# Linear attention with a gated layer behind it: the state's sum written in place in PSUM, the last three output steps in another order, and the last gate's product on VectorE

## The chip, the cores and the metric

The kernel runs on one core of a Trainium2 chip. The metric is the device time of one execution in microseconds, as the median of several. Five engines work beside each other, each with its own queue: TensorE (PE) multiplies matrices into PSUM, VectorE (DVE), ScalarE (ACT) and GpSimd (POOL) work element by element, and SyncE (SP) issues the DMAs. In this kernel GpSimd's operands all lie in SBUF; VectorE's and ScalarE's lie in SBUF or in PSUM.

## The reference, cut to what matters

B, H, S, D are 4, 8, 768, 48. The first part is a linear attention with a decaying state, the second a gated layer with a spatial mix over the sequence.

```python
state = zeros(B, H, D, D)
for t in range(S):
    cur = einsum('bhd,bhe->bhde', u[None] * kt, vt)
    y[:, :, t] = einsum('bhd,bhde->bhe', rt, state + cur)
    state = w[None, :, :, None] * state + einsum('bhd,bhe->bhde', kt, vt)
x = y.transpose(0, 2, 1, 3).reshape(B, S, H * D)          # 4 x 768 x 384

h = maximum(x @ w_in, 0.0)                                # 384 -> 1024
u, v = h[..., :512], h[..., 512:]
v_n = (v - mean(v)) / sqrt(var(v) + 1e-06)
v_s = einsum('ts,bsd->btd', w_spatial, v_n) + b_spatial[None, :, None]
out = (u * v_s) @ w_out                                   # 512 -> 384
```

## The kernel before, in words

**Attention.** Each of the 4 batches is cut into 6 chunks of 128 time steps, 24 chunks in all (`NM`), and each chunk into two halves of 64. Every chunk goes through these steps. `prep` (lines 237 to 275) scales r and k by powers of w: `scale` (L248 on GpSimd, L249 on VectorE; from chunk 8 on L251 on VectorE alone), `rku` and `ks` on GpSimd (L254, L255, L258), a sum over features `red` on VectorE (L261), and `dia` on GpSimd (L270). `g1` (L287, L296) makes on TensorE the products of k and r and of k and v into the PSUM tile `ps`, of which there is one buffer (two banks). `mid` (lines 306 to 327) takes the masked products out on VectorE (L310) and carries the state on: `ua` and `ub_` are the k-v products of the two halves, views of `ps`. L318 adds `ua` to the state `s` into `t1`, L325 adds `ub_`, and L326 multiplies by `w128`, which gives the state of the next chunk; the tile of each is 128 x 4 x 48 float32. ScalarE copies the state and `t1` into block form (L303, L304), which `g2` (L336) on TensorE uses to make the chunk's output. `fin` and `fin_low` (L366 on ScalarE, then either L376 on TensorE and L377 on ScalarE, or L368 on VectorE) split it into a high and a low part.

**The layer behind it.** Every product is made of three matmuls on high and low parts (`mm3`, L392 to L394): high by high, high by low, low by high. `moe_v` and `moe_u` make the two halves of the hidden layer, `moe_sp` mixes over the sequence and makes the gate, `moe_out` multiplies by w_out. In `moe_sp`, VectorE adds the bias (L479), GpSimd multiplies by u (L480), and then ScalarE and VectorE split the gate into a high and a low part (`split`, L172 and L173). In `moe_out`, 4 feature blocks of 3 matmuls each (12 in all) fill one PSUM tile `pm`, ScalarE copies it into the SBUF tile `ob` (L492), and SP stores it (L493). `pm` has four buffers, and `ob` has two.

**The order of the work.** Every engine runs its instructions in the order in which the program writes them out; no planner changes it. The loop at the end of `fused_kernel` (lines 542 to 587) writes, for each chunk, `g2`, `fin`, `g1` of the next chunk, `mid` of the next chunk, the loads of the chunk three further on, `prep` of the chunk two further on, and between these the steps of the layer from the list `steps` and pieces of the weights' preparation from the list `fill` (`pour`). In the first chunks (i < 6) the counts in `FIRST` and `POUR` say how many steps and pieces. The pieces (`from_f64`, lines 175 to 205) turn raw 64-bit weights into two float32 parts, mostly on VectorE (L183 to L203) with one copy on ScalarE (L200); `sp_pieces` does the same for the spatial weights. `later` and `tick` put a function behind so many steps; a gate's `split` follows its `moe_sp` at once. The last steps of the last batch (b = 3, t = 1) are the four `moe_sp` and then three `moe_out`, for 128 rows of the output each.

Of the kernel before, what the change touches and what calls it, by code (L numbers as in the profile page):

```python
# [7 lines left out]
F32 = mybir.dt.float32  # L8
# [3 lines left out]
ALU = mybir.AluOpType  # L12
AX = mybir.AxisListType

B, H, S, D = 4, 8, 768, 48
# [3 lines left out]
P = 128  # L19
# [4 lines left out]
NP = H // 2  # L24
NK = DM // P
NS = S // P
ND = DH // P
# [9 lines left out]
def fused_kernel(ctx, tc, rkT, rkvN, wT, uB, w_in, w_sp, b_sp, w_out, out):  # L37
    nc = tc.nc
# [16 lines left out]
    ps_m = ctx.enter_context(tc.tile_pool(name="ps_m", bufs=4, space=bass.MemoryType.PSUM))  # L55
# [15 lines left out]
    def raw_out(k):  # L71
        t = sm.tile([P, 2 * DM], U32, name="raw", tag="gt", bufs=5)
        raws["out", k] = t.rearrange("p (n k) -> p n k", k=2)
        src = w_out[k * P:(k + 1) * P, :]
        nc.sync.dma_start(out=raws["out", k], in_=src.bitcast(U32).rearrange("p (n k) -> p n k", k=2))

    def raw_sp(t, j):
        if t == 0:
            w = sm.tile([P, TH], F32, name="wst", tag="u", bufs=8)
        else:  # L80
            w = sm.tile([P, TH], F32, name="wst", tag="ob")
        raws["sp", t, j] = w
        nc.sync.dma_start(out=w, in_=w_sp[j * P:(j + 1) * P, t * TH:(t + 1) * TH])
# [40 lines left out]
    w128 = const.tile([P, NP], F32, name="w128")  # L124
# [27 lines left out]
    for n in range(2):  # L152
        t = const.tile([P, 2, NP, HC], F32, name=f"a{n}")
# [3 lines left out]
    for n in range(2):  # L157
        t = const.tile([P, NP, 2 * D], F32, name=f"sb{n}")
# [12 lines left out]
    def split(hi, lo, src, eng=None):  # L171
        nc.scalar.copy(hi, src)  # L172
        (eng or nc.vector).tensor_tensor(out=lo, in0=src, in1=hi.bitcast(F32), op=ALU.subtract)  # L173
# [128 lines left out]
    def block(dst, src):  # L302
        nc.scalar.copy(dst[0:64, :, 0:D], src[0:64])  # L303
        nc.scalar.copy(dst[64:P, :, D:2 * D], src[64:P])  # L304

    def mid(m):
        t, c = at[m], m % NC
        ps = t["ps"]
        ua, ub_ = (ps[:, i, 256:256 + NP * D].rearrange("p (n e) -> p n e", n=NP) for i in (1, 0))
        nc.vector.copy_predicated(out=t["a"], mask=mask_u.unsqueeze(1).unsqueeze(1).to_broadcast([P, 2, NP, HC]),  # L310
                                  data=ps[:, :, 0:256].rearrange("s j (p t) -> s j p t", p=NP))
        if c == 0:
            block(sblk[1], ua)
            t1 = ua
        else:
            block(sblk[0], st["s"])
            t1 = sm.tile([P, NP, D], F32, name="t1", bufs=1)
            nc.vector.tensor_tensor(out=t1, in0=st["s"], in1=ua, op=ALU.add)  # L318
            block(sblk[1], t1)
        if c < NC - 1:  # L320
            if c == 0:
                t1 = sm.tile([P, NP, D], F32, name="t1", bufs=1)
                nc.vector.tensor_copy(out=t1, in_=ua)
            s2 = sm.tile([P, NP, D], F32, name="s2")
            nc.vector.tensor_tensor(out=s2, in0=t1, in1=ub_, op=ALU.add)  # L325
            nc.vector.tensor_tensor(out=s2, in0=s2, in1=w128.unsqueeze(2).to_broadcast([P, NP, D]), op=ALU.mult)  # L326
            st["s"] = s2

    def g2(m):
        t, c = at[m], m % NC  # L330
        xp = ps_x.tile([P, 2, 512], F32, name="xp")
        t["xp"] = xp
        began = set()

        def mm(z, g, jt, lhsT, rhs):
            nc.tensor.matmul(xp[32 * g:32 * g + 32, z, jt * HC:(jt + 1) * HC], lhsT, rhs, start=(z, g) not in began,  # L336
                             stop=True, skip_group_check=True, tile_position=(ROWP[0], 32 * g))
            began.add((z, g))

        quads = [(jt, g, *((jt, g) if g < 3 else (3, jt))) for jt in range(NK) for g in range(4)]  # L340
        ROWP = [0]
        for z, s0, t0 in SUBS:
            if z == 0 and c == 0:
                continue
            for jt, g, p, k in quads:
                mm(z, g, jt, sblk[z][:, p, 32 * k:32 * k + 32], t["r"][:, p, t0:t0 + 64])
        parts = []
        for jt, g, p, k in quads:
            if k < 2:
                parts.append((jt, g, p, 0, 32 * k))  # L350
            if k > 0:
                parts.append((jt, g, p, 1, 32 * (k - 1)))
        for jt, g, p, j, e in parts:
            for z, s0, t0 in SUBS:
                ROWP[0] = s0
                mm(z, g, jt, t["v"][s0:s0 + 64, 2 * p + j, e:e + 32], t["a"][s0:s0 + 64, j, p, :])
# [25 lines left out]
    def later(n, f):  # L382
        due.setdefault(now[0] + n, []).append(f)

    def tick():
        now[0] += 1
        for f in due.pop(now[0], []):
            f()


    def mm3(o, lh, ll, rh, rl, first, last):
        nc.tensor.matmul(o, lh, rh, start=first, stop=False)  # L392
        nc.tensor.matmul(o, lh, rl, start=False, stop=False)  # L393
        nc.tensor.matmul(o, ll, rh, start=False, stop=last)  # L394
# [76 lines left out]
    def moe_sp(b, t, d):  # L471
        ds_ = slice(d * P, (d + 1) * P)
        ts_ = slice(t * TH, (t + 1) * TH)
        pm = ps_m.tile([P, 512], F32, name="pm")
        for s, vn in enumerate(vst[b]):
            mm3(pm[:, 0:TH], vn[:, 0, ds_], vn[:, 1, ds_], ws_h[:, s, ts_], ws_l[:, s, ts_], s == 0, s == NS - 1)
        u = us.pop((b, t, d))
        g = sm.tile([P, TH], F32, name="g", bufs=2)
        nc.vector.tensor_tensor(out=g, in0=pm[:, 0:TH], in1=bb[:, ts_], op=ALU.add)  # L479
        nc.gpsimd.tensor_tensor(out=g, in0=g, in1=u, op=ALU.mult)  # L480
        gt = sm.tile([P, 2, TH], F32R, name="gt", tag="gt", bufs=5)
        gs[b, t, d] = gt
        later(1, lambda: split(gt[:, 0], gt[:, 1], g))

    def moe_out(b, t, i):
        pm = ps_m.tile([P, 512], F32, name="pm")
        o = slice(i * P, (i + 1) * P)
        for d in range(ND):
            gt = gs[b, t, d]
            mm3(pm[:, 0:DM], gt[:, 0, o], gt[:, 1, o], wo_h[:, d, :], wo_l[:, d, :], d == 0, d == ND - 1)  # L490
        ob = sm.tile([P, DM], F32, name="ob", tag="ob")
        nc.scalar.copy(ob, pm[:, 0:DM])  # L492
        nc.sync.dma_start(out=out[b, t * TH + i * P:t * TH + (i + 1) * P, :], in_=ob)  # L493
# [3 lines left out]
    for b in range(B):  # L497
        v = [(moe_v, (b, c)) for c in range(NC)]
        u = [(moe_u, (b, t, d)) for t in range(2) for d in range(ND)]
# [30 lines left out]
    def pour(n):  # L530
        for _ in range(max(0, min(n, len(fill)))):
            fill.pop(0)()

    def sp_loads(t):
        for j in range(NS if t == 0 else 2):
            raw_sp(t, j)
        if t == 0:
            nc.sync.dma_start(out=bb, in_=b_sp)

    DMAS = {0: lambda: sp_loads(0), 2: lambda: [raw_out(k) for k in range(ND)], 3: lambda: sp_loads(1)}  # L540
    done = 0
    for i in range(-1, NM):
        if i < 0:
            parts = prep(0)
            for f in parts[0:2]:
                f()
            pour(4)
            for f in parts[2:]:
                f()
        else:  # L550
            g2(i)
            xs_all[divmod(i, NC)[0], i % NC // 3], *low = fin(i)
        if i < NM - 1:
            g1(i + 1)
        if i >= 0:
            fin_low(i, *low)
        if i < NM - 1:
            mid(i + 1)
        if i >= 0:
            load_chunk(i + 3)  # L560
        parts = prep(i + 2) if i < NM - 2 else []
        n = 0 if i < 0 else FIRST[i] if i < NC else len(steps) if i == NM - 1 else int(10 + (i - 5) * 28 / 6)
        p = POUR[i + 1] if i + 1 < len(POUR) else (0, len(fill))
        if i < NC:
            for _ in range(2):
                parts.pop(0)()
            pour(p[0])
            for f in parts:
                if f:
                    f()  # L570
            parts = []
        k = max(1, n - done)
        for j in range(k):
            pour(p[1] * (j + 1) // k - p[1] * j // k)
            if parts:
                parts.pop(0)()
            if done < n:
                f, args = steps[done]
                whole = {moe_v: 18, moe_u: 36, moe_sp: 42 if args[1] == 0 else 48, moe_out: 72}[f]
                pour(whole - 72 + len(fill))  # L580
                f(*args)
                done += 1
                tick()
        for f in parts:
            f()
        if i in DMAS:
            DMAS[i]()
    for _ in range(6):
        tick()

# [49 lines left out]
```

## Time and profile before

| | us |
|---|---|
| median of 3 runs (lowest, highest) | 379.31 (378.53, 379.43) |
| the profiled execution, its own time | 379.35 |
| its span, from the first to the last instruction | 377.5 |
| TensorE busy | 342.9 |
| VectorE busy | 215.9 |
| GpSimd busy | 152.5 |
| ScalarE busy | 145.3 |

The busy times are sums over the span; an engine that waits is not busy. A row of the time line gives an instruction's start and its duration, both in us, its engine, its line, what it writes and reads, and in brackets how long the engine had been idle and who ended that. A VectorE instruction's duration runs on while it is held up in the middle of its work, so two instructions of one shape and line can differ. Matmuls overlap: their starts, not their durations, say how fast they follow each other. "issue" is time for which the profile shows no other engine to wait for.

### The profile page before, as it was taken

The numbers are of one execution on the slowest core, as the hardware profiler recorded it, in microseconds if no ns is written. First come the engines' busy times: TensorE is split into PE (matmuls) and PEld (weight loads), VectorE is DVE, ScalarE is ACT, GpSimd is POOL, SyncE is SP. The second block draws the span as 40 slices with busy tenths as digits, with TensorE's granted clock in tenths as the row PEclk, the third lists the DMA queues.
The fourth block names the chain that finished last, engine by engine and source line by source line (L and its number), as shares of the span: only waits on it lengthen the run. The fifth ranks groups of instructions, "written<-read, shape, count | busy, mean of one in ns | idle before, by whom it ended". The sixth has DMA issues, their size and how long they took to land.

```text
span 377.5 us, 12269 instructions
## 1 busy us (share of the span) xinstructions
PE 342.9 (91%) x5459; PEld 314.1 (83%) x5459; DVE 215.9 (57%) x415; ACT 145.3 (38%) x320; POOL 152.5 (40%) x157
## 2 busy tenths in 40 slices
PE   2467669698999999999999999999999999999995
PEld 1456548597999998789899999889989998999994
DVE  6699975687855464577644445597444534443120
ACT  3033455756322333547313223647122335461212
POOL 5865745656265353421445273241563330003120
PEclk9996957989999999999999999999999999999999
DMA  7992933233303235303305314334031010000101
GB/s 260 417 387 92 322 144 130 82 129 129 129 2 129 73 129 180 120 20 133 115 2 180 110 71 152 128 104 150 5 127 65 4 44 25 0 0 2 42 21 64
DMA packets 14021, 41.69 MB, mean 110 GB/s; under 512 B 1680, under 2 KB 6416, under 8 KB 13968
## 3 DMA queue, kind: packets, MB, share of 16 engines
q1 hardware_dynamic: 13968, 40.90, 30.6%
q8 instruction: 43, 0.70, 0.8%
q14 instruction: 10, 0.08, 0.1%
HBM read 36.18 MB, written 4.72 MB: 108 GB/s over the span
## 4 chain that ended last, share of the span: by engine, by line
PE 81%; DVE 7%; DMA 3%; ACT 3%; issue 3%; POOL 2%; SPq 0%; POOLq 0%; DVEq 0%; ACTq 0%
PE pm L392 21%; PE pm L394 20%; PE pm L393 20%; PE xp L336 9%; PE ps L287 3%; PE ps L296 3%; DMA rkv<-rkvN 2%; DMA wst<-w_sp 2%; DVE rk L249 1%; PE pm L462 1%; PE pm L467 1%; PE pm L463 1%; DVE pm L199 1%; ACT vs L436 1%; DVE s L326 1%
## 5 line engine op out<-in xcount | busy, mean ns | idle before, releaser
L480 POOL TENSOR_TENSOR g<-g,u 128x384 f32<-128x384 f32 x32 | 32.5, 1016 | 118.0 <-DVE g L479 118.0
L392 PE MATMUL pm<-ws_h,vnorm 128*128 128x384 f32 x192 | 64.9, 338 | 0.0
L394 PE MATMUL pm<-ws_h,vnorm 128*128 128x384 f32 x192 | 64.2, 335 | 0.0
L393 PE MATMUL pm<-ws_l,vnorm 128*128 128x384 f32 x192 | 64.2, 334 | 0.0
L270 POOL TENSOR_TENSOR a<-diag,dg 128x512 f32<-128x512 f32 x24 | 25.4, 1059 | 86.0 <-DVE dg L261 56.1
L173 DVE TENSOR_TENSOR gt<-g,gt 128x384 fp32r<-128x384 f32 x32 | 21.0, 655 | 57.8 <-ACT gt L172 57.8
L172 ACT CAST gt<-g 128x384 fp32r<-128x384 f32 x32 | 16.4, 513 | 91.7 <-POOL g L480 91.7
L392 PEld LDWEIGHTS pm<-ws_h,vnorm 128*128 128x128 f32 x192 | 36.0, 188 | 0.3
L393 PEld LDWEIGHTS pm<-ws_l,vnorm 128*128 128x128 f32 x192 | 36.1, 188 | 0.0
L394 PEld LDWEIGHTS pm<-ws_h,vnorm 128*128 128x128 f32 x192 | 36.0, 188 | 0.0
L392 PE MATMUL pm<-wo_h,gt 128*128 128x384 f32 x96 | 33.0, 344 | 0.8 <-ACT gt L172 0.8
L394 PE MATMUL pm<-wo_h,gt 128*128 128x384 f32 x96 | 32.5, 338 | 0.4 <-issue 0.4
L393 PE MATMUL pm<-wo_l,gt 128*128 128x384 f32 x96 | 32.3, 336 | 0.0
L393 PE MATMUL pm<-wi_l,xh 128*128 128x512 f32 x72 | 29.6, 411 | 0.9 <-issue 0.9
L392 PE MATMUL pm<-wi_h,xh 128*128 128x512 f32 x72 | 30.2, 419 | 0.0
L394 PE MATMUL pm<-wi_h,xl 128*128 128x512 f32 x72 | 29.4, 408 | 0.0
L479 DVE TENSOR_TENSOR g<-pm,bb 128x384 f32<-128x384 f32 x32 | 17.7, 554 | 19.9 <-PE pm L394 19.8
L255 POOL TENSOR_TENSOR rkv<-rkv,ub 128x384 f32<-128x384 f32 x24 | 26.2, 1092 | 1.9
L336 PEld LDWEIGHTS xp<-rk,sb 128*32 128x32 f32 x1056 | 18.2, 118 | 9.8 <-issue 4.5
L413 DVE BATCH_NORM_STATS2 q<-vs 128x6 f32<-128x512 f32 x24 | 16.5, 687 | 16.6 <-ACT vs L406 16.6
L336 PE MATMUL xp<-a,rkv 64*32 64x64 f32 x1536 | 25.0, 234 | 0.0
L336 PE MATMUL xp<-rk,sb 128*32 128x64 f32 x1056 | 23.1, 234 | 2.1 <-ACT sb L303 2.1
(102 smaller groups left out, 733.7 us busy)
## 6 DMA issues: line engine op xcount, KB each, us to landing
rkv<-rkvN SPq DMA_DIRECT2D x24, 648.0 KB, 5.7
rk<-rkT SPq DMA_DIRECT2D x24, 512.0 KB, 4.1
out<-ob SPq DMA_DIRECT2D x24, 192.0 KB, 1.9
raw<-w_in SPq DMA_DIRECT2D x6, 512.0 KB, 9.9
wst<-w_sp SPq DMA_DIRECT2D x12, 192.0 KB, 6.7
raw<-w_out SPq DMA_DIRECT2D x4, 384.0 KB, 7.3
bb<-b_sp SPq DMA_DIRECT2D x1, 384.0 KB, 5.6
ub<-uB SPq DMA_DIRECT2D x1, 192.0 KB, 6.6
```

The source lines that it names most:

```text
L172: nc.scalar.copy(hi, src)
L173: (eng or nc.vector).tensor_tensor(out=lo, in0=src, in1=hi.bitcast(F32), op=ALU.subtract)
L255: nc.gpsimd.tensor_tensor(out=rn, in0=rn, in1=ub, op=ALU.mult)
L270: nc.gpsimd.tensor_tensor(out=a.rearrange("s j p t -> s (j p) t"), in0=diag.unsqueeze(1).to_broadcast([P, H, HC]), in1=dg.rearrange("s j p ...
L287: nc.tensor.matmul(ps[s0:s0 + 64, j, p * HC:(p + 1) * HC], t["k"][hd, p, s0:s0 + 64], t["r"][hd, p, t0:t0 + 64], start=True, stop=True, sk ...
L336: nc.tensor.matmul(xp[32 * g:32 * g + 32, z, jt * HC:(jt + 1) * HC], lhsT, rhs, start=(z, g) not in began, stop=True, skip_group_check=Tru ...
L392: nc.tensor.matmul(o, lh, rh, start=first, stop=False)
L393: nc.tensor.matmul(o, lh, rl, start=False, stop=False)
L394: nc.tensor.matmul(o, ll, rh, start=False, stop=last)
L413: nc.vector.bn_stats(out=q6[:, c % 3, :], in_=vs)
L479: nc.vector.tensor_tensor(out=g, in0=pm[:, 0:TH], in1=bb[:, ts_], op=ALU.add)
L480: nc.gpsimd.tensor_tensor(out=g, in0=g, in1=u, op=ALU.mult)
```

## The change

Three things change; a fourth is only written in another way.

1. In `mid`, the sum of `t1` and `ub_` is written over `ub_` in PSUM instead of into the SBUF tile `s2`, and the multiplication by `w128` reads it from there and writes `s2`.
2. For the last batch's second half, the three `moe_out` steps become one: three `pm` tiles are taken, feature blocks 0 to 2 are multiplied for all three, then block 3 for each, with the copy and the store of each behind its block 3.
3. For the last gate alone, the product with u goes to VectorE instead of GpSimd.
4. The table `DMAS` of loads behind chunks 0, 2 and 3 becomes the function `bulk`, with the same loads in the same places.

```diff
             s2 = sm.tile([P, NP, D], F32, name="s2")
-            nc.vector.tensor_tensor(out=s2, in0=t1, in1=ub_, op=ALU.add)
-            nc.vector.tensor_tensor(out=s2, in0=s2, in1=w128.unsqueeze(2).to_broadcast([P, NP, D]), op=ALU.mult)
+            nc.vector.tensor_tensor(out=ub_, in0=t1, in1=ub_, op=ALU.add)
+            nc.vector.tensor_tensor(out=s2, in0=ub_, in1=w128.unsqueeze(2).to_broadcast([P, NP, D]), op=ALU.mult)
             st["s"] = s2
...
-        nc.gpsimd.tensor_tensor(out=g, in0=g, in1=u, op=ALU.mult)
+        (nc.vector if (b, t, d) == (B - 1, 1, ND - 1) else nc.gpsimd).tensor_tensor(out=g, in0=g, in1=u, op=ALU.mult)
...
     def moe_out(b, t, i):
+        if (b, t) == (B - 1, 1):
+            if i == 0:
+                pms = [ps_m.tile([P, 512], F32, name="pm") for _ in range(3)]
+                for d0, d1 in ((0, ND - 1), (ND - 1, ND)):
+                    for k in range(3):
+                        out_sum(b, t, k, pms[k], d0, d1)
+                        if d1 == ND:
+                            out_end(b, t, k, pms[k])
+            return
         pm = ps_m.tile([P, 512], F32, name="pm")
+        out_sum(b, t, i, pm, 0, ND)
+        out_end(b, t, i, pm)
+
+    def out_sum(b, t, i, pm, d0, d1):
         o = slice(i * P, (i + 1) * P)
-        for d in range(ND):
+        for d in range(d0, d1):
             gt = gs[b, t, d]
             mm3(pm[:, 0:DM], gt[:, 0, o], gt[:, 1, o], wo_h[:, d, :], wo_l[:, d, :], d == 0, d == ND - 1)
+
+    def out_end(b, t, i, pm):
         ob = sm.tile([P, DM], F32, name="ob", tag="ob")
         nc.scalar.copy(ob, pm[:, 0:DM])
         nc.sync.dma_start(out=out[b, t * TH + i * P:t * TH + (i + 1) * P, :], in_=ob)
```

## Rows read from the trace of the kernel before

**Rows 1.** The page, TensorE's granted clock in 40 slices, in tenths of full speed.
```profile
PEclk9996957989999999999999999999999999999999
```
**Rows 2.** Table of stretches: span, busy us and instructions per engine, granted clock, DMA.
```profile
20.00:40.00 20.00, 13.62 (x365) 10.77 (x365) 19.59 (x32) 6.45 (x16) 12.33 (x12) 0.83 0.63 228
...
120.00:377.50 257.50, 251.14 (x3616) 235.35 (x3614) 126.60 (x249) 96.02 (x208) 84.77 (x84) 1.00 0.22 76
```
**Rows 3.** Time line of VectorE in the first 90 us: start us, duration us, instruction.
```profile
15.36 0.95 DVE L326 TENSOR_TENSOR s<-s,w 128x192 f32<-128x192 f32 x1
16.23 1.48 DVE L249 TENSOR_TENSOR rk<-rk,tt 128x512 f32<-128x512 f32 x1
...
31.57 0.71 DVE L326 TENSOR_TENSOR s<-s,w 128x192 f32<-128x192 f32 x1
...
76.64 0.89 DVE L326 TENSOR_TENSOR s<-s,w 128x192 f32<-128x192 f32 x1
...
88.54 1.16 DVE L326 TENSOR_TENSOR s<-s,w 128x192 f32<-128x192 f32 x1
```
**Rows 4.** Time line of GpSimd beside these.
```profile
15.09 1.00 POOL L255 TENSOR_TENSOR rkv<-rkv,ub 128x384 f32<-128x384 f32 x1
16.05 1.11 POOL L258 TENSOR_TENSOR rkv<-rkv,tn 128x384 f32<-128x384 f32 x1
20.04 1.04 POOL L270 TENSOR_TENSOR a<-diag,dg 128x512 f32<-128x512 f32 x1 [2.88 <-DVE dg L261]
...
31.07 1.00 POOL L255 TENSOR_TENSOR rkv<-rkv,ub 128x384 f32<-128x384 f32 x1
```
**Rows 5.** VectorE's groups by shape (busy us, mean ns); for L249 min/median/max ns.
```profile
L326 DVE TENSOR_TENSOR s<-s,w 128x192 f32<-128x192 f32 x20 | 10.5, 525 | 0.7
L325 DVE TENSOR_TENSOR s<-t,ps 128x192 f32<-128x192 f32 x20 | 7.1, 354 | 0.7
L199 DVE TENSOR_TENSOR pm<-pm,hb 128x512 f32<-128x512 f32 x6 | 4.1, 690 | 0.1
L203 DVE TENSOR_TENSOR wi_l<-pm,wi_h 128x512 fp32r<-128x512 f32 x6 | 4.1, 684 | 0.8 <-ACT wi_h L200 0.7
L249 DVE TENSOR_TENSOR rk<-rk,tt x8: 677/692/1492, 5.5 to 77.5; 128x512 f32<-128x512 f32 x8
```
**Rows 6.** Chain of waits that ended last: start us, length us, what it is.
```profile
45.16 2.68 issue
```
**Rows 7.** Time line of TensorE: idle time before it, and who ended it, in brackets.
```profile
28.18 0.50 PE L287 MATMUL ps<-rk 64*64 64x64 f32 x18 [1.26 <-issue]
...
40.27 0.47 PE L376 MATMUL xp<-xh,neg 128*128 128x192 f32 x2 [1.17 <-ACT xh L366]
...
88.35 0.47 PE L376 MATMUL xp<-xh,neg 128*128 128x192 f32 x2 [1.36 <-ACT xh L366]
```
**Rows 8.** Time line of TensorE in the tail, the last three output steps.
```profile
366.52 0.34 PE L392 MATMUL pm<-wo_h,gt 128*128 128x384 f32 x1
...
367.91 0.34 PE L394 MATMUL pm<-wo_h,gt 128*128 128x384 f32 x1
369.02 0.44 PE L392 MATMUL pm<-wo_h,gt 128*128 128x384 f32 x1 [0.78 <-ACT gt L172]
...
373.89 0.34 PE L394 MATMUL pm<-wo_h,gt 128*128 128x384 f32 x1
```
**Rows 9.** Time lines of VectorE, GpSimd and ScalarE in the tail.
```profile
366.72 0.56 DVE L479 TENSOR_TENSOR g<-pm,bb 128x384 f32<-128x384 f32 x1 [0.25 <-PE pm L394]
...
367.42 1.01 POOL L480 TENSOR_TENSOR g<-g,u 128x384 f32<-128x384 f32 x1 [2.09 <-DVE g L479]
...
374.31 0.48 ACT L492 COPY ob<-pm 128x384 f32<-128x384 f32 x1 [1.60 <-PE pm L394]
```
**Rows 10.** The stores of L493 over the whole run, and one earlier copy into `ob`.
```profile
DMA to landing us min/median/max: 1.8/1.9/3.3
...
126.08 0.48 ACT L492 COPY ob<-pm 128x384 f32<-128x384 f32 x1 [1.61 <-DMA out<-ob]
```

More of the change, by code (lines that the diff above doesn't have):

```diff
@@ L538, in sp_loads, with bulk @@
             nc.sync.dma_start(out=bb, in_=b_sp)
-    DMAS = {0: lambda: sp_loads(0), 2: lambda: [raw_out(k) for k in range(ND)], 3: lambda: sp_loads(1)}
+    def bulk(i):
+        if i == 0:
+            sp_loads(0)
+        if i == 2:
+            for k in range(ND):
+                raw_out(k)
+        if i == 3:
+            sp_loads(1)
     done = 0
@@ L585, in fused_kernel @@
             f()
-        if i in DMAS:
-            DMAS[i]()
+        bulk(i)
     for _ in range(6):
```

## The prediction, made before the result was known

> **What bounds the kernel now.** I read a table of stretches first, with the granted clock beside it, then VectorE and GpSimd side by side in the first 100 us, then the chain of waits, and last the tail. From 120 us on TensorE is busy for 251.14 of 257.50 us at full granted clock [rows 2], so there nothing on another engine is worth anything unless TensorE waits for it. The first 100 us are different: between 20 and 40 us TensorE is busy for 13.62 of 20 us, at 0.83 of its clock, and VectorE for 19.59 of 20 [rows 2]. There VectorE is the bound: it turns the raw weights into two halves and runs the state's recurrence between them, and the chain of waits runs through it until TensorE's L376 at 40.27, which waits for ScalarE's L366 [rows 7].
>
> What slows VectorE there is to be seen in one instruction. L326 (the multiplication of the state's sum by w128) has 20 executions and 10.5 us in all, a mean of 525 ns; L325, the addition before it, of the same 128x192 shape, takes 354 ns each time [rows 5]. The excess, 20 x (525 - 354) = 3.4 us, is not spread: six executions hold it, 5.5 us together, of which four stand in [rows 3] (0.95, 0.71, 0.89 and 1.16 us); the other 14 take (10.5 - 5.5) / 14 = 0.357 us. Beside GpSimd's rows the cause is plain: L326 begins at 15.36 while GpSimd's L255 runs from 15.09 to 16.09, and ends at 16.31, just behind it; at 31.57 L255 runs to 32.07, and L326 ends at 32.28 [rows 3, 4]. So an instruction of VectorE whose two inputs both lie in SBUF waits until the GpSimd instruction that is running ends. The next one, L249, has two SBUF inputs too: it starts behind L326, meets GpSimd's next instruction L258 (16.05 to 17.16), and takes 1.48 us where its median is 0.69 [rows 3 to 5]. The addition L325 has one input in PSUM, and its 20 executions are alike.
>
> **The change part by part.** *The state's sum in PSUM.* One addition now writes over ub_ in PSUM instead of s2 in SBUF, and the multiplication reads it there. Counts stay the same (20 each). Neither form stands in the trace with this shape, so I bound the price of the PSUM accesses from neighbours. L199 reads PSUM and SBUF and writes PSUM: 690 ns for 512 columns. L203 reads PSUM and SBUF and writes SBUF: 684 ns [rows 5]. So a write to PSUM costs between 0 and 6 ns here, and a read of PSUM beside SBUF between -3 and 0 (L325 at 354 ns against the L326 that isn't held, 357). I take nothing; with 20 pairs the bounds are -0.1 and +0.1 us.
>
> A rule speaks against this edit: the Trainium skill (Perfetto Trace Analysis, "Optimizing Scalar/DVE Operations") puts the access overhead of a VectorE operation at about 60 ns on SBUF and about 125 ns on PSUM. By that page the two instructions would cost some 130 ns more for each sum, an estimate, and with three sums on the path the forecast would be 0.4 us later. The trace does not agree: 690 against 684 ns.
>
> What it saves: L326 then has only w128 in SBUF, as L325 has only t1, and should take 0.36 us whatever GpSimd does. L249 then comes early, while L255 still runs, and takes the turn that L326 had. I work this out at the first place. L326 runs from 15.36 to 15.72, L249 is there at 15.64 (16.23 lies 0.08 before L326's end too), L255 ends at 16.09. L249's part after a release is 17.71 - 17.16 = 0.55 us (it was held to the end of L258), so it ends at 16.64 instead of 17.71: 1.07 us of VectorE's time, made of L326's own 0.59 and of the wait for L258. The same pattern stands at three places (15.36, 23.79 and 31.57; the first and the last of the three are in [rows 3, 4]), each 1.07 us, 3.2 in all. At the fourth, at 42.78, VectorE has 0.7 us to spare soon after and I count nothing. L258 starts later by L249's 0.55 us; GpSimd's next instruction, L270, waits for VectorE anyway (2.88 us at the first place [rows 4]), and TensorE's matmuls on L258's product come behind those on L249's, so this is hidden; without that cover it would cost up to 0.55 us at each place.
>
> What is late next? Behind the second place, TensorE: it stops for 1.26 us in L287 before 28.18, with nothing in the profile to wait for [rows 7], and VectorE's L310 at 30.19 needs the matmuls that follow. I let that stop move with TensorE's own work and take 0.1 us off: 3.1. Then the chain goes from VectorE over L200 and L366 on ScalarE to TensorE's L376 at 40.27; TensorE idles 1.17 us before it [rows 7], and its own work has moved 2.1 us by then, so 3.1 us gets through. From 45.16 TensorE stops again for 2.68 us without a releaser [rows 6]; I let that move as a whole. At 76.64 the multiplication loses 0.53 us, of which L249 behind it takes 0.3 over; the 0.2 left is on ScalarE's path to the matmul at 88.35, which waits 1.36 us for it [rows 3, 7]. At 88.54 VectorE gains 0.8 us [rows 3], but of the matmul that waits for it in the end, at 92.06, TensorE's own work would let only 0.2 us go. These two small terms lie between 0 and 1.3 us together. Sum of this part: 3.1 + 0.2 + 0.2 = 3.5 us. ps has one buffer and is now held until the end of L326 instead of L325, 0.4 us longer. The next matmuls into it (L287) read what L249 makes, and L249 stands behind L326 on the same engine, so they can't come sooner in the early chunks; later a whole stage of TensorE lies between. Cost nothing; without that, 0.4 us a chunk. s2 is written once instead of twice, with the same readers.
>
> *The last output steps.* Now nine matmuls cover the last gate, from 366.52 to the ninth's start at 367.91, (367.91 - 366.52) / 8 = 0.174 us apart; the tenth starts at 369.02 and the 36th at 373.89 [rows 8]. Thirty-six in a row would start their last at 366.52 + 35 x 0.174 = 372.60: 1.3 us are lost. With 27 in front, block 3 is wanted at 366.52 + 27 x 0.174 = 371.2, while TensorE takes the gate's first half at 369.02 even with the product on GpSimd. So TensorE gains the 1.3 us.
>
> But the stores do not. Tile ob has two buffers. Now the copies L492 stand twelve matmuls, 2.08 us, apart, so the third finds the first buffer free. After the change they could start at 371.98, 372.50 and 373.02 (three matmuls, 0.52 us, apart, and each 0.42 us behind the start of its last matmul, as 374.31 is behind 373.89 [rows 8, 9]), and the third must wait for the first store. This wait is in the trace where three copies come together: the third stood 1.61 us for the store [rows 10]. Here: the first copy ends at 372.46 (0.48 us), its store is 1.9 us to landing in the median (least 1.8 [rows 10]), 374.36; the third copy begins at about 374.4 instead of 374.31. So the tail's gain is 0, or a loss of 0.1; bounds: -1.3 if the third copy needn't wait, +0.5 if the two stores slow each other (their longest took 3.3). I take +0.1. Behind the waiting copy nothing else is queued on ScalarE, and on SP only its own store.
>
> *The last product on VectorE.* 0.56 us (L479's row, same shape) instead of GpSimd's 1.01 [rows 9], in the shadow of 18 matmuls more: nothing; without that cover, a gain of about 0.5 us. *The DMAS table as a function* issues the same DMAs in the same places: nothing.
>
> Sum: the profiled execution took 379.35 us (span 377.5, 1.85 around it), and the median of the runs is 379.31. 379.35 - 3.5 + 0.1 = 375.95, say 376.0.
>
> **The rivals.** *A turn is lost to GpSimd.* L249 must be waiting before L255 ends. The room is 16.09 - 15.64 = 0.45 us at the first place and 32.07 - 31.85 = 0.2 at the third [rows 3, 4]. If GpSimd's L258 goes first there, the chunk gains nothing on L249's end. One or two places lost: 377.1 to 378.2. For it: the small room, and the 0.1 us that TensorE takes off. Against it: at 15.36 the waiting L326 went ahead of L258. The Trainium skill (SBUF — State Buffer, "Who interferes with whom") says that whoever issues first gets the shared port for its whole instruction and the other blocks. The trace agrees, with the ends 16.31 behind 16.09.
>
> *VectorE's gain is swallowed.* If TensorE's stops at 28.18 and 45.16 stay where they are in time, the chain goes on from 47.84 as before: 379.4. For it: the stops have no releaser in the profile, and DMA is busy around both. Against it: they stand inside runs of the same small matmuls (L287), which moves with the work.
>
> *Slower: the clock.* In four early slices the granted clock is 0.6, 0.5, 0.7 and 0.8 [rows 1]; the drops follow idle time of TensorE. Earlier work can meet a low stretch that now falls into a wait. A slice is 9.4 us; one more at 0.5 with matmuls queued throughout costs 4.7 us, against 3.5 gained and 0.1 lost: 379.35 + 1.3 = 380.7. It decides from the point where over 3.4 us of matmul time are lost, that is 7 us more at half clock. Against it: less waiting makes TensorE idle less.
>
> *The third copy needn't wait* (a store that frees its buffer sooner): 374.7.
>
> **How the numbers follow.** Forecast 376.0, its own range 375.0 to 377.0: 0.50. A turn lost: 0.20. Swallowed: 0.16. Slower by the clock: 0.08. Tail gains too: 0.06. About 0.3% (1.1 us) is what a measurement of this kernel can tell from no change. Faster is the forecast, the lost turn and the tail: 0.76; the same is the swallowed gain: 0.16; slower 0.08. To leave out no more than 2 in 10 the range must reach the swallowed case: 374.5 to 379.5.
>
> **What would show it.** Right: all 20 executions of the multiplication near 0.36 us; L249 at the three places at about 1.0 us instead of 1.48; L376 of 40.27 near 37.2; the third copy waiting for a store, about 1.3 us; TensorE's last matmul 1.3 us nearer to its first of the tail, and the end not. Wrong: a multiplication that is still held, L249 still at 1.48 us, a third copy with no wait, or a TensorE stop that stays at its time and hands on nothing.

## The result, and the profile after

| kernel | us, median of its runs (lowest, highest) | against the kernel before, 95% interval |
|---|---|---|
| before | 379.24 (378.53, 379.43) | |
| after | 375.69 (374.47, 376.11) | 0.9911 (0.9892 to 0.9931) |

The changed kernel is 3.4 us faster (0.0089 x 379.24). Its profiled execution took 376.00 us with a span of 374.3, where the one before took 379.35 with 377.5. These groups of VectorE's instructions answer to [rows 5]; the columns are the same (busy us, mean ns, then the idle time before).

```profile
L326 DVE TENSOR_TENSOR s<-ps,w 128x192 f32<-128x192 f32 x20 | 7.1, 357 | 0.7
L325 DVE TENSOR_TENSOR ps<-t,ps 128x192 f32<-128x192 f32 x20 | 7.3, 363 | 0.7
```

The multiplication, 525 ns in the mean before, now takes 357, and its 20 executions lie between 356 and 359 ns. The addition, which now writes PSUM, went from 354 to 363. The time line of VectorE at the first three places answers to [rows 3].

```profile
15.36 0.36 DVE L326 TENSOR_TENSOR s<-ps,w 128x192 f32<-128x192 f32 x1
15.63 0.99 DVE L249 TENSOR_TENSOR rk<-rk,tt 128x512 f32<-128x512 f32 x1
...
22.98 0.83 DVE L249 TENSOR_TENSOR rk<-rk,tt 128x512 f32<-128x512 f32 x1
...
29.18 0.74 DVE L310 COPY_PREDICATED a<-mask,ps 128x512 f32<-128x512 uint32 x1 [1.05 <-PE ps L296]
...
30.86 0.68 DVE L249 TENSOR_TENSOR rk<-rk,tt 128x512 f32<-128x512 f32 x1
```

GpSimd's at the first place, to [rows 4]:

```profile
15.08 1.00 POOL L255 TENSOR_TENSOR rkv<-rkv,ub 128x384 f32<-128x384 f32 x1
16.03 1.45 POOL L258 TENSOR_TENSOR rkv<-rkv,tn 128x384 f32<-128x384 f32 x1
```

TensorE's, to [rows 6, 7]:

```profile
20.52 0.36 PE L376 MATMUL xp<-xh,neg 128*128 128x192 f32 x2 [2.20 <-issue]
...
27.30 0.79 PE L287 MATMUL ps<-rk 64*64 64x64 f32 x18 [1.22 <-issue]
...
38.12 0.74 PE L376 MATMUL xp<-xh,neg 128*128 128x192 f32 x2 [2.40 <-ACT xh L366]
...
45.61 0.39 PE L287 MATMUL ps<-rk 64*64 64x64 f32 x11 [1.18 <-issue]
```

At the first place L249 ends at 15.63 + 0.99 = 16.62, where it ended at 16.23 + 1.48 = 17.71: 1.09 us sooner, and GpSimd's L258, which now comes second, takes 1.45 us instead of 1.11. At the second it ends at 23.81 instead of 25.96: another 1.06. At the third it ends at 31.54 instead of 33.69: 2.15 us sooner, exactly what the first two had brought, and the third adds nothing. VectorE stands idle there for 1.05 us, ahead of L310, for TensorE. TensorE's L376 of 40.27 now starts at 38.12, 2.15 us sooner.

In the tail, TensorE's time line answers to [rows 8].

```profile
363.06 0.34 PE L392 MATMUL pm<-wo_h,gt 128*128 128x384 f32 x1
...
369.12 0.34 PE L394 MATMUL pm<-wo_h,gt 128*128 128x384 f32 x1
```

ScalarE's answers to [rows 9]:

```profile
368.50 1.00 ACT L507 COPY ob<-pm 128x384 f32<-128x384 f32 x2 [3.55 <-PE pm L394]
370.98 0.48 ACT L507 COPY ob<-pm 128x384 f32<-128x384 f32 x1 [1.48 <-DMA out<-ob]
```

TensorE's 36 matmuls run without a hole, 6.06 us from the first start to the last instead of 7.37 (366.52 to 373.89). The third copy waits 1.48 us for a store, and starts 7.92 us behind the first matmul instead of 7.79. So all of the gain, 366.52 - 363.06 = 3.46 us, is there when the tail begins, and the tail gives 0.13 back.

### The profile page after: what moved, and what is told of

Its sections match the earlier page's. It is cut to its first block, busy times and chain, and to the rows that moved or that the text cites. A ratio compares the mean times of both kernels' runs of the same rounds, so it can differ in the third digit from the quotient of the medians.

```text
span 374.3 us, 12268 instructions
## 1 busy us (share of the span) xinstructions
PE 340.6 (91%) x5459; PEld 313.5 (84%) x5459; DVE 213.6 (57%) x416; ACT 145.3 (39%) x320; POOL 151.6 (40%) x156
## 4 chain that ended last, share of the span: by engine, by line
PE 81%; DVE 6%; ACT 5%; issue 3%; DMA 2%; POOL 1%; SPq 0%; DVEq 0%; ACTq 0%
PE pm L392 21%; PE pm L393 20%; PE pm L394 20%; PE xp L336 10%; PE ps L287 4%; PE ps L296 3%; DMA rkv<-rkvN 2%; ACT vs L436 1%; DVE rk L249 1%; ACT vnorm L438 1%; PE xp L376 1%; DVE a L310 1%; PE pm L462 1%; PE pm L467 1%; PE pm L463 1%
## 5 line engine op out<-in xcount | busy, mean ns | idle before, releaser
L480 POOL TENSOR_TENSOR g<-g,u 128x384 f32<-128x384 f32 x31 | 31.5, 1017 | 115.4 <-DVE g L479 115.4
L255 POOL TENSOR_TENSOR rkv<-rkv,ub 128x384 f32<-128x384 f32 x24 | 26.2, 1092 | 1.9
L258 POOL TENSOR_TENSOR rkv<-rkv,tn 128x384 f32<-128x384 f32 x24 | 25.4, 1060 | 0.0
L254 POOL TENSOR_TENSOR rkv<-rkv 128x384 f32<-128x384 f32 x24 | 24.2, 1010 | 2.2 <-DMA rkv<-rkvN 2.2
```

What stands on the lines that cost most here:

```text
L254: nc.gpsimd.tensor_tensor(out=rn, in0=rn, in1=kn, op=ALU.mult)
L255: nc.gpsimd.tensor_tensor(out=rn, in0=rn, in1=ub, op=ALU.mult)
L258: nc.gpsimd.tensor_tensor(out=kn, in0=kn, in1=tn_f, op=ALU.mult)
L480: (nc.vector if (b, t, d) == (B - 1, 1, ND - 1) else nc.gpsimd).tensor_tensor(out=g, in0=g, in1=u, op=ALU.mult)
```

## The experiments

My theory after the comparison: VectorE gains where a multiplication was held by GpSimd, and the tail's gain is eaten by the two buffers of ob. Against it stood that the tail carries a part, that the gain comes from writing s2 only once, and that the third place gave nothing for a reason that could be taken away. All ratios are to runs of the kernel before on the same chip.

**The sum alone.** The diff's first part, nothing else.

```diff
-            nc.vector.tensor_tensor(out=s2, in0=t1, in1=ub_, op=ALU.add)
-            nc.vector.tensor_tensor(out=s2, in0=s2, in1=w128.unsqueeze(2).to_broadcast([P, NP, D]), op=ALU.mult)
+            nc.vector.tensor_tensor(out=ub_, in0=t1, in1=ub_, op=ALU.add)
+            nc.vector.tensor_tensor(out=s2, in0=ub_, in1=w128.unsqueeze(2).to_broadcast([P, NP, D]), op=ALU.mult)
```

> Only the state's sum goes to PSUM; the output steps and the last gate's product stay as they were. Theory (the gain is VectorE's, in the first 100 us, and the tail gives back what TensorE gains): 375.6 to 376.0, that is 3.3 to 3.6 us under the kernel before; multiplication at 0.36 us in all 20 executions; the tail from its first matmul on w_out to the third copy as before, 7.79 us. Rival (the tail carries part of the gain, about 1.3 us): 377.1.

Measured: 375.98 us, ratio 0.9916 (0.9900 to 0.9931), the ratio of the whole change. The tail is the old one, 363.26 to 371.04, 7.78 us.

**The tail alone.** The other parts of the diff, with the sum in SBUF.

> Only the last three output steps in the new order and the last product on VectorE; the sum stays in SBUF. Theory: 379.3, within 0.3 us of the kernel before; the third copy waits some 1.5 us for the first store, and from the first matmul on w_out to the third copy it is 7.9 us against 7.79. Rival (the order is worth what TensorE no longer waits): 378.0.

Measured: 379.24 us beside 378.92, ratio 1.0002 (0.9993 to 1.0012). The third copy waits 1.48 us for a store and starts 374.26 - 366.34 = 7.92 us behind the first matmul, as in the changed kernel. The reordering is worth nothing by itself.

**A third buffer.** The changed kernel, in which the third copy gets a tile of u, of the same size and long free.

```diff
     def out_end(b, t, i, pm):
-        ob = sm.tile([P, DM], F32, name="ob", tag="ob")
+        if (b, t, i) == (B - 1, 1, 2):
+            ob = sm.tile([P, DM], F32, name="ob", tag="u", bufs=8)
+        else:
+            ob = sm.tile([P, DM], F32, name="ob", tag="ob")
```

> The changed kernel, with a free buffer of the tile u for the third output copy. Theory (the third copy waits for the first store's landing and for nothing else): the copy begins about 1.4 us sooner, 0.42 us behind its last matmul's start, and the time is 374.3, 1.4 us under the changed kernel. Rival (the stores share something and land one behind the other): the third store lands later behind its issue than 1.9 us and less than 0.7 us is gained.

ScalarE's time line in the tail of this kernel:

```profile
369.16 1.48 ACT L510 COPY ob<-pm 128x384 f32<-128x384 f32 x3 [3.55 <-PE pm L394]
```

The three copies follow each other without a wait: the third ends at 370.64, 6.92 us behind the first matmul (363.72), where in the changed kernel it ended 8.40 us behind it (371.46 - 363.06). That is 1.48 us. From the third copy's end to the end of the span it is 2.9 us here (373.5) and 2.8 in the changed kernel (374.3), so the rival, stores that hold each other up, did not come. The time was 374.52 us, ratio 0.9889 (0.9873 to 0.9904), 0.8 us below the changed kernel's 0.9911; the two intervals overlap, so by these times alone the gain can be anything from nothing to more than the 1.4 us expected.

**The first two places alone.** The sum goes to PSUM for chunks 0 and 1.

```diff
+            sum_ = ub_ if m in (0, 1) else s2
-            nc.vector.tensor_tensor(out=s2, in0=t1, in1=ub_, op=ALU.add)
-            nc.vector.tensor_tensor(out=s2, in0=s2, in1=w128.unsqueeze(2).to_broadcast([P, NP, D]), op=ALU.mult)
+            nc.vector.tensor_tensor(out=sum_, in0=t1, in1=ub_, op=ALU.add)
+            nc.vector.tensor_tensor(out=s2, in0=sum_, in1=w128.unsqueeze(2).to_broadcast([P, NP, D]), op=ALU.mult)
```

> The sum goes to PSUM for chunks 0 and 1 only (the multiplications at 15.36 and 23.79 of the kernel before), tail as before. Theory (each of the two gives 1.07 us, and the third place gives nothing since VectorE then waits for TensorE): VectorE's L249 of the third place ends about 2.1 us sooner than before, the time is 376.6 to 377.2. Rival A (the three places add up, 1.07 each, as predicted): 377.1 with a third place that is still held, and the changed kernel's rest comes from it. Rival B (the gain comes later, at 76 to 92 us): 379.

VectorE's time line of this kernel at the third place and behind it (the new line moves L326 to L327):

```profile
29.96 0.74 DVE L310 COPY_PREDICATED a<-mask,ps 128x512 f32<-128x512 uint32 x1 [1.77 <-PE ps L296]
...
31.36 0.36 DVE L327 TENSOR_TENSOR s<-s,w 128x192 f32<-128x192 f32 x1
31.63 0.68 DVE L249 TENSOR_TENSOR rk<-rk,tt 128x512 f32<-128x512 f32 x1
...
41.41 1.00 DVE L327 TENSOR_TENSOR s<-s,w 128x192 f32<-128x192 f32 x1
...
48.72 0.97 DVE L327 TENSOR_TENSOR s<-s,w 128x192 f32<-128x192 f32 x1
```

377.39 us, ratio 0.9956 (0.9940 to 0.9972), 1.7 us, less than expected. The third place missed its forecast too: L249 ends there at 31.63 + 0.68 = 32.31, 1.38 us sooner than in the kernel before and not 2.1. At this place the multiplication has both inputs in SBUF and still isn't held: VectorE waits 1.77 us for TensorE and comes so late that GpSimd is past it. The multiplications of the fourth and fifth chunk are held, for 1.00 and 0.97 us. The fifth took 0.36 us before (at 50.91), but the freed places need not have moved that: it took 0.70 us with the tail alone and 0.97 with another tile in SBUF (below), where nothing is freed ahead of it. A hold depends on where the two engines stand to each other, and that differs between executions too.

**The later places alone.** The same edit with chunks 2, 3, 6 and 7.

> The sum goes to PSUM for chunks 2, 3, 6 and 7 only (the multiplications at 31.57, 42.78, 76.64 and 88.54 of the kernel before), tail as before. Theory (what a place gives depends on whether VectorE or TensorE is late there; with the first two places untouched VectorE is the late one at the third): L249 of the third place ends about 1.07 us sooner than its 33.69, and the time is 377.3 to 377.9, 1 to 1.6 us under the kernel before, so that this and the first two together give more than the changed kernel has. Rival (only the first two places carry anything): 378.8.

376.73 us, ratio 0.9953 (0.9939 to 0.9967), 1.8 us. Here VectorE is the late one at the third place, and the place pays: L249 ends at 31.83 + 0.74 = 32.57, 1.12 us sooner than its 33.69. Together with the first two the sum is 1.7 + 1.8 = 3.5 us, as much as the sum alone gave (3.2, interval 2.6 to 3.8), not more; that the two groups would overlap, as I had expected, isn't measured.

**Another tile in SBUF.** The sum goes to a tile of its own, and s2 is written once.

```diff
+            s3 = sm.tile([P, NP, D], F32, name="s3")
-            nc.vector.tensor_tensor(out=s2, in0=t1, in1=ub_, op=ALU.add)
-            nc.vector.tensor_tensor(out=s2, in0=s2, in1=w128.unsqueeze(2).to_broadcast([P, NP, D]), op=ALU.mult)
+            nc.vector.tensor_tensor(out=s3, in0=t1, in1=ub_, op=ALU.add)
+            nc.vector.tensor_tensor(out=s2, in0=s3, in1=w128.unsqueeze(2).to_broadcast([P, NP, D]), op=ALU.mult)
```

> The sum goes to a tile of its own in SBUF, and the multiplication reads it there and writes s2: s2 is written once, as in the changed kernel, but nothing goes to PSUM. Theory (two inputs in SBUF are what makes VectorE wait for GpSimd): six multiplications still take 0.7 to 1.2 us, the time is the kernel before's, 378.9. Rival (the gain comes from s2 being written only once, at its end): 375.9.

VectorE's group of the multiplication in this kernel:

```profile
L327 DVE TENSOR_TENSOR s<-s,w 128x192 f32<-128x192 f32 x20 | 10.3, 516 | 0.7
```

Still 516 ns in the mean, and 378.82 us beside 378.77, ratio 1.0002 (0.9991 to 1.0013). It isn't the number of writes to s2; it is where the multiplication's input lies.

**GpSimd's two instructions left out.** The kernel before, without L255 and L258 of chunk 1.

```diff
-            nc.gpsimd.tensor_tensor(out=rn, in0=rn, in1=ub, op=ALU.mult)
+            if m != 1:
+                nc.gpsimd.tensor_tensor(out=rn, in0=rn, in1=ub, op=ALU.mult)
...
-            nc.gpsimd.tensor_tensor(out=kn, in0=kn, in1=tn_f, op=ALU.mult)
+            if m != 1:
+                nc.gpsimd.tensor_tensor(out=kn, in0=kn, in1=tn_f, op=ALU.mult)
```

> The kernel before, with GpSimd's two multiplications L255 and L258 of chunk 1 left out (that part of chunk 1 is not computed); the sum stays in SBUF. Theory (VectorE waits for the GpSimd instruction that runs beside it): the first multiplication by w128 at 15.4 takes 0.36 us instead of 0.95, and L249 behind it 0.69 us instead of 1.48; the later held ones stay held. Rival (the multiplication waits for something of its own): 0.95 us as before.

VectorE's time line at the first two places (L326 is L328 here):

```profile
15.42 0.36 DVE L328 TENSOR_TENSOR s<-s,w 128x192 f32<-128x192 f32 x1
15.70 0.68 DVE L249 TENSOR_TENSOR rk<-rk,tt 128x512 f32<-128x512 f32 x1
...
22.45 0.78 DVE L328 TENSOR_TENSOR s<-s,w 128x192 f32<-128x192 f32 x1
23.15 1.48 DVE L249 TENSOR_TENSOR rk<-rk,tt 128x512 f32<-128x512 f32 x1
```

With both inputs in SBUF and no GpSimd beside them, the two take 0.36 and 0.68 us; one chunk later, where GpSimd runs again, 0.78 and 1.48. So it is GpSimd that holds them. The Trainium skill (SBUF — State Buffer, "Who interferes with whom") says that a VectorE instruction with two SBUF inputs contends with a GpSimd instruction that reads SBUF, and that one with at most one, outside VectorE's 2-port modes, does not; these rows and the 20 undisturbed multiplications after the change agree. (The one execution of this kernel took 376.49 us; its result is not the kernel's, so nothing is read from the time.)

**The loads of w_out later.** The changed kernel, `if i == 2` made `if i == 4` ahead of the four `raw_out`.

> The changed kernel, with the four loads of w_out issued behind chunk 4 instead of chunk 2; they are first read at about 80 us. Theory (TensorE's stop at about 44 us is a fetch of instructions that queues behind these loads): the stop of 1.18 us falls under 0.5 us and the time goes down by 0.3 to 0.8 us, to about 375.2. Rival (the stop is a fixed price of that place in the program): it stays at 1.1 to 1.3 us, 375.7.

379.19 us, ratio 1.0018 (1.0007 to 1.0029): slower by 4 us than the changed kernel. The loads, 1.5 MB, now stand ahead of a load of the spatial weights, and ScalarE waits for that:

```profile
81.44 0.51 ACT L172 CAST ws_h<-wst 128x384 fp32r<-128x384 f32 x1 [3.69 <-DMA wst<-w_sp]
```

So the time says nothing of the question. The stop says something:

```profile
43.75 0.39 PE L287 MATMUL ps<-rk 64*64 64x64 f32 x11 [0.99 <-issue]
```

Its 0.99 us look like the changed kernel's 1.18, between the theory's 0.5 and the rival's 1.1 to 1.3. But TensorE came to it at 43.75 - 0.99 = 42.76, 1.67 us sooner. In one execution of the kernel with a third buffer and the product on GpSimd (below), where these loads are in their old place, TensorE came at 42.86 and stopped for 2.02 us; the DMA's share from 42 to 43 us was 1.03 there and is 0.48 here. So, as far as two executions show it, these loads made about 1 us of the stop, and the other 1 us isn't theirs.

**The early loads later.** The changed kernel, with `raw_in` of 3 to 5 behind chunk 0 and `sp_loads(0)` behind chunk 1.

> The changed kernel, with the last three loads of raw w_in (first read at about 32 us) behind chunk 0 instead of in front, and the spatial weights' loads (first read at about 52 us) behind chunk 1. Theory (TensorE's stops before 20.52 and 27.30 are fetches of instructions behind these loads, and they are why the third place gives nothing): the stop before 20.52 falls from 2.20 us to under 1.3 us, VectorE no longer waits 1.05 us for TensorE before its L310 at 29.18, and the time is about 374.9. Rival (the stops don't depend on the loads): 2.2 and 1.2 us as now, 375.7.

TensorE's time line (two lines fewer: L374 is L376, L301 is L303, L285 is L287, L308 is L310, L294 is L296):

```profile
19.05 0.36 PE L374 MATMUL xp<-xh,neg 128*128 128x192 f32 x2 [0.46 <-ACT xh L364]
...
22.76 1.24 PE L334 MATMUL xp<-rk,sb 128*32 128x64 f32 x24 [1.63 <-ACT sb L301]
...
27.20 0.80 PE L285 MATMUL ps<-rk 64*64 64x64 f32 x18 [1.12 <-issue]
```

VectorE's, at the third place:

```profile
29.08 0.74 DVE L308 COPY_PREDICATED a<-mask,ps 128x512 f32<-128x512 uint32 x1 [0.98 <-PE ps L294]
```

375.93 us, ratio 0.9929 (0.9909 to 0.9948), not distinct from the changed kernel. The stop before 20.52, 2.20 us, is gone. In the eight other executions with the sum of the first two places in PSUM, the changed kernel's among them, this L376 starts between 20.41 and 21.12; here it starts at 19.05. So the stop did come from these loads, though the run doesn't tell which of the two groups. But nothing follows: TensorE now waits 1.63 us for ScalarE's copies of the state instead, the next stop is still 1.12 us, and VectorE waits 0.98 us where it waited 1.05. My theory of the third place, and with it the 374.9 us expected, fell with this. The first stop was hidden behind VectorE's own state.

**The product on GpSimd.** The third buffer's kernel with the last product on GpSimd, as it was.

> The changed kernel with the free third buffer, but the last gate's product on GpSimd as before the change. Theory (the product lies in the shadow of 27 matmuls): 374.5, as with the product on VectorE, within 0.2 us; TensorE's 36 matmuls on w_out follow each other without a hole. Rival (the product is on the path once the buffer isn't): 375.0.

373.89 us, ratio 0.9870 (0.9849 to 0.9892), against 0.9889 with the product on VectorE. TensorE's 36 matmuls took 6.07 us in both, so the difference lay elsewhere; I ran the two again on one chip.

> The changed kernel with the free third buffer, the last product on VectorE, again, beside the same with the product on GpSimd on one chip. Theory (the product is in the shadow, and the 0.6 us between the two earlier runs came from the first 80 us of different executions): both within 0.3 us, 374.0 to 374.5, and 6.07 us from the start of the first matmul on w_out to that of the last. Rival (the product on GpSimd is better): this one 0.6 us slower.

> The same with the last product on GpSimd. Theory: within 0.3 us of the one with it on VectorE, 374.0 to 374.5, 6.07 us from the first to the last matmul on w_out. Rival: 0.6 us faster.

374.61 us, ratio 0.9885 (0.9867 to 0.9903), and 374.72 us, ratio 0.9879 (0.9857 to 0.9900): the same. The product's place is worth nothing either way. The third buffer is the fastest version: four sets of runs, two with either place of the product, give ratios of 0.9870 to 0.9889, 4.2 to 4.9 us under the kernel before. That it also beats the changed kernel rests on the four together and on the 1.48 us in the trace; each set's interval alone reaches the changed kernel's (0.9892 to 0.9931).

## Why the prediction was right, and which of its steps was not

*The time.* 376.0 was forecast, and 375.69 measured. Where VectorE is held, the turn that L249 takes at the first two places, and the tail came as worked out. One term of the sum, the third place, was 0.95 us too large, and gains of 0.36 and 0.49 us that stand nowhere in the sum made up for most of it; that the total fits so well is luck.

*What bounds the kernel, and the hold:* right. Without GpSimd's two instructions the hold is gone; with another SBUF tile it stays.

*The price of PSUM:* nearly right. The write cost 363 - 354 = 9 ns, where I had bounded it at 6 from L199 and L203, and the read nothing. The Trainium skill's figures (Perfetto Trace Analysis, "Optimizing Scalar/DVE Operations") would have been, by an estimate, some 125 - 60 = 65 ns more for each access; the trace does not agree.

*L249's turn, 1.07 us a place:* right at the first (1.09) and the second (1.06). The rival that a turn is lost to GpSimd did not come: L249 went ahead at both, and L258 took 1.45 us. That L258's delay is hidden held too: nothing behind it came later.

*What is late next, 3.1 us through to L376:* this step failed. I let TensorE's stop before 28.18 move with TensorE's work and took 0.1 us off. 2.15 us came through, not 3.1. The stop ended 0.88 us sooner (27.30), but the 18 matmuls behind it took 0.79 us instead of 0.50, and TensorE finished what L310 reads at 29.03 (27.93 + 1.10), hardly sooner than the 29.20 before. VectorE waited 1.05 us, passed GpSimd's instructions unheld, and was no further than the first two places had brought it.

The step is weaker still than this pair of traces shows. With the first two places held, the stop ended at 28.18 in the kernel before, and at 27.51, 27.72 and 27.71 in three others (tail alone, another tile, later places). With them freed, it ended between 27.18 and 28.07 in nine executions. TensorE came to it 1.05 us sooner in the mean (26.08 against 27.13 us), and it ended only 0.3 us sooner (27.49 against 27.78). So at this stop the rival of the swallowed gain, a stop that stays where it is in time, holds for the larger part.

Was it the slower matmuls? Up to the tail, the runs with a third buffer are the same program as the changed kernel, and they show both cases. In the one with the product on GpSimd the 18 matmuls took 0.50 us at the same place:

```profile
27.18 0.50 PE L287 MATMUL ps<-rk 64*64 64x64 f32 x18 [1.14 <-issue]
...
37.98 0.47 PE L376 MATMUL xp<-xh,neg 128*128 128x192 f32 x2 [1.91 <-ACT xh L366]
...
44.88 0.39 PE L287 MATMUL ps<-rk 64*64 64x64 f32 x11 [2.02 <-issue]
```

VectorE's time line of that kernel:

```profile
28.35 0.73 DVE L310 COPY_PREDICATED a<-mask,ps 128x512 f32<-128x512 uint32 x1 [0.26 <-PE ps L296]
29.74 0.36 DVE L326 TENSOR_TENSOR s<-ps,w 128x192 f32<-128x192 f32 x1
30.02 1.38 DVE L249 TENSOR_TENSOR rk<-rk,tt 128x512 f32<-128x512 f32 x1
```

And GpSimd's:

```profile
28.88 1.00 POOL L255 TENSOR_TENSOR rkv<-rkv,ub 128x384 f32<-128x384 f32 x1
29.84 1.00 POOL L258 TENSOR_TENSOR rkv<-rkv,tn 128x384 f32<-128x384 f32 x1
```

VectorE waits only 0.26 us and reaches L310 0.83 us sooner than in the changed kernel. But now L249 comes at 30.02, when L255 has ended and L258 has begun at 29.84; it is held to L258's end at 30.84 and takes 1.38 us. It ends at 31.40, against 31.54 in the changed kernel. This is the rival of the lost turn, at the place where I had given it 0.2 us of room: the 0.26 us of waiting for TensorE use it up. So the third place gives nothing on either way: late, VectorE isn't held; early, it loses the turn; and L376 comes at 37.98 or 38.12. All nine executions with the first two places freed do one or the other: in three VectorE waits 0.26 to 0.36 us and L249 takes 1.25 to 1.38, in six it waits 0.98 to 1.77 us and L249 takes 0.68.

*The stop at 45.16 moves as a whole:* wrong. Before, TensorE came to it at 45.16, and it ended at 47.84; in the changed kernel the two are 44.43 (45.61 - 1.18) and 45.61, so the arrival moved by 0.73 us and the end by 2.23. In the four runs with a third buffer, the same program that far, TensorE came at 42.86 (the one just shown), 43.10, 43.54 and 44.54, and the stop ended at 44.88, 45.62, 45.24 and 45.53. With the changed kernel's, the arrivals lie 1.7 us apart and the ends 0.7: in the main, a TensorE that comes later finds a shorter stop, and so the stop swallows much of what is lost ahead of it. The loads of w_out have a part in its end, as the run with late loads showed. What sets the rest was not found; that it is a fetch of instructions, as two expectations supposed, no run shows.

*The two small terms, 0.2 us each:* right. The matmul of 88.35 came at 85.58 and that of 92.06 at 89.09, 2.77 and 2.97 us sooner, where L376 of 74.11 was 2.51 sooner (71.60). The first step is 0.26, the second 0.20.

*From 120 us on nothing is worth anything:* not quite. Between 92 us and the tail the shift grew from 2.97 to 3.46 us. TensorE has three stops there without a releaser, 1.1, 0.9 and 0.4 us before; after, there are two, of 1.4 and 0.6. I had not counted them.

So the sum was 3.5 us by 3.1 + 0.2 + 0.2, and the measured 3.46 by 2.15 up to the third place, 0.36 more by 74 us (2.51 - 2.15), 0.46 for the two small terms, and 0.49 behind 92 us. These are readings of one execution each. In the five other executions whose program is the same up to the tail (the sum alone, and the four with a third buffer), the matmul of 74.11 comes at 70.81 to 72.20, so a term of a few tenths can differ as much between executions.

*The tail:* right in each step. The copy waited 1.48 us where I had 374.4 - 373.0 = 1.4, and it starts 0.13 us later against the first matmul where I had 0.1. The third buffer shows that nothing else stood behind it. *The product and the table of loads:* nothing, as said.

## What to carry to other kernels

When one VectorE instruction of a shape takes 0.36 us in most executions and twice that in a few, lay GpSimd's time line beside it before looking for anything else, and count also what the next instruction loses by the turn. Put one of two SBUF inputs into PSUM where it lies there anyway: the price was 9 ns, and a hold cost up to 0.8 us. When a reordering closes a hole on TensorE, ask at once how far apart the results now come and how many buffers take them: the store's landing, 1.9 us, took back the 1.3 us that the order had won until a third buffer was there.

## What the runs showed that I had not expected

A hold wanders. With the first two places freed, the third was no longer held although its inputs lay in SBUF. The fifth took 0.36 us in the kernel before and 0.70 and 0.97 us in two kernels that free nothing. So what a place is worth can't be read from one trace: the third gave nothing when the first two were freed with it, and 1.1 us when they were not.

TensorE's stops without a releaser are not fixed prices. The changed kernel's stop before 20.52 fell from 2.20 us to nothing when 3.1 MB of loads (3 x 512, 6 x 192 and 384 KB) were issued later, and the one at 45 us is 2.68 us long before and 1.18 after.

Nor is the clock a constant of a stretch. This is the table of stretches of the changed kernel (span, then TensorE, its loads, VectorE, ScalarE and GpSimd busy, then the granted clock and the DMA's share and rate):

```profile
18.00:21.00 3.00, 0.68 (x26) 0.57 (x17) 2.96 (x6) 0.91 (x3) 2.05 (x2) 1.00 1.03 406
25.00:30.00 5.00, 3.62 (x89) 3.10 (x75) 3.88 (x8) 1.04 (x4) 4.31 (x5) 0.50 1.04 373
```

The same stretches of the kernel with a third buffer and the product on GpSimd, which is the same program up to the tail:

```profile
18.00:21.00 3.00, 1.17 (x34) 1.12 (x27) 2.97 (x6) 0.99 (x3) 2.08 (x2) 1.00 1.03 408
25.00:30.00 5.00, 2.91 (x87) 2.34 (x76) 4.60 (x9) 1.28 (x3) 4.35 (x5) 0.84 1.01 383
```

And of the changed kernel with the early loads later:

```profile
18.00:21.00 3.00, 1.66 (x58) 1.35 (x53) 2.97 (x6) 1.88 (x5) 2.06 (x2) 1.00 0.80 263
25.00:30.00 5.00, 3.65 (x88) 3.13 (x75) 3.95 (x7) 1.04 (x4) 4.33 (x5) 0.50 0.93 318
```

The first two kernels differ by nothing that has run by then, and yet the clock of the second stretch is the lower level (0.50, 1.2 GHz) in one and mostly the higher in the other (0.84; 1.00 is 2.4 GHz). In the first, TensorE had stopped for longer shortly before (2.20 us against 1.60). That invites a simple reading, that the longer stop brought the lower clock. The third kernel speaks against it: it has no such stop, and has the lower clock too. Why it fell there is open. Nor does the granted clock always tell how fast the matmuls go. In the second execution of the kernel with a third buffer and the product on GpSimd it is 1.00 in the second stretch, and yet the 18 matmuls take 0.80 us, as at 0.50:

```profile
25.00:30.00 5.00, 3.46 (x99) 3.02 (x86) 3.43 (x7) 1.08 (x3) 4.23 (x5) 1.00 1.05 390
...
27.82 0.80 PE L287 MATMUL ps<-rk 64*64 64x64 f32 x18 [1.54 <-issue]
```

So a clock row is to be read beside the matmuls' own times.
